# Fewer bursts of zero matmuls, wider routing steps, and two reorderings in an attention-then-experts kernel

## The chip, the cores and the metric

One core of a Trainium2 chip. The metric is device time in microseconds (us). The kernel before took 813.58 us (median of 4 runs, 812.43 to 816.94) beside the changed one. Later runs were on other chips, where the same kernel before took 829.9, 811.6 and 817.0 us; kernels are compared within one chip, or by their ratios to the kernel before on their own chip. Ratios are the mean time of one kernel's fast runs over that of the other's of the same rounds, so not quite the ratio of the medians quoted.

## The reference

```python
# q, k, v: (8 batches, 8 heads, 576 positions, 64)
scores = q @ k.T / 8                 # heads 0-3: last 32 positions; heads 4-7: every 4th of the last 128
attn = softmax(masked scores) @ v    # -> x: (8, 576, 512)
logits = x @ w_gate                  # 8 experts
local  = sigmoid(x @ w_local)
for each batch, for s in order:
    e = argmax(logits[s]) if s == 0 or local[s] < 0.5 else previous e
    out[s] = softmax(logits[s])[e] * (relu(x[s] @ w1[e]) @ w2[e])
```

The choice of an expert is carried from one position to the next, so the routing of a group of two batches is a chain of small steps. The 4608 tokens are then sorted by expert into tiles of 128.

## The kernel before

TensorE's order is set by the program; the other engines' instructions are placed by a scheduler. An outer loop goes over 32 pairs of heads: scores on TensorE (`sc`), a clamp with the mask on VectorE and an exponential on ScalarE (`pr`), value matmuls (`pv`), a scaling on VectorE (`x`), and after every second pair nine transposes (`tp`). A pair's values have 32 positions in common with the block before; VectorE copies them inside the tile once its load has landed (`overlap`). After eight pairs a group is routed: logits, then small steps, each started when a counter of TensorE's work in us (`gap`) has moved on far enough. Forty expert tiles follow.

```python
def overlap(n):
    vt = loaded[n][2]
    nc.vector.tensor_copy(vt[:WIN, :, 1:], vt[QB:, :, :NB - 1])

def idle(times):                 # a burst: products of zeros that nobody reads
    to = bank([P, 4, P], "idle")
    for i in range(times):
        nc.tensor.matmul(to, lhsT=blank, rhs=blank..., start=True, stop=True, ...)

def route(g):
    waiting.extend((us, lambda f=f: f(g)) for us, f in (
        (0.0, logits), (1.5, fresh), (4.0, carry), (1.5, carry_over), (1.0, choose), (2.0, place)))
    # ... table, nine scatters of table entries by GpSimd, then for a table: rows, four tokens() ...

for n in range(NPB + 2):
    if n % 4 == 2 and not begun[0]:   # begun: the experts have
        idle(4)
    if n < NPB:
        scores(n)
        overlap(n)
    gap(1.2); step()                  # step: a part of an expert tile, if one is ready
    if 1 <= n <= NPB:
        values(n - 1) ...
    # ... turn (transposes), load(n + 3), two weight pieces, store ...
```

The logits of a group use three 32-column strips of the array, 384 positions each; the middle strip's positions come from two batches, so its 384 are two runs of 192, and the second of them came in a second round.

Of the kernel before, what the change touches and what calls it, by code (L numbers as in the profile page):

```python
# [22 lines left out]
P = 128  # L23
B, H, S, DH = 8, 8, 576, 64
D = H * DH
E, F = 8, 1024
DK, FK = D // P, F // P
N = B * S
WIN, DIL = 32, 4
# [8 lines left out]
NPB = B * NP  # L38
# [3 lines left out]
CH = 2  # L42
# [3 lines left out]
GB = 2  # L46
NG = B // GB
# [3 lines left out]
NC = 3  # L51
NQ = GS // NC
LW = 32
# [9 lines left out]
NT = CAP + E - 1  # L63
PADS = E * CAP
NOBODY = float(N)

TW = 4

# [121 lines left out]
def whole(ctx, tc, exact, bad, qk, v, wgl, w1, w2, con, msk, qmk, out, cst, wg, ones):  # L190
    nc = tc.nc
# [20 lines left out]
    def bank(shape, name):  # L212
        return banks.tile(shape, F32, name=name, tag="bank")
# [14 lines left out]
    def load(n):  # L228
        kq = ins.tile([P, WIN + 2 * S], F32, name="kq")
        vt = vts[n % len(vts)]  # L230
        nc.sync.dma_start(out=kq, in_=qk[n])
        nc.sync.dma_start(out=vt[WIN:].rearrange("p u i e -> p (u i e)"), in_=v[n])
        loaded[n] = kq[:, :WIN + S], kq[:, WIN + S:], vt
# [5 lines that stand above are left out]
# [5 lines left out]
    def idle(times):  # L244

        if not exact:
            to = bank([P, 4, P], "idle")
            for i in range(times):
                nc.tensor.matmul(to, lhsT=blank, rhs=blank.unsqueeze(1).to_broadcast([P, 4, P]), start=True, stop=True, skip_group_check=True)  # L249
# [18 lines left out]
    nc.vector.memset(fill, 0.0)  # L268
    nc.vector.memset(fill[:, :, 0], NOBODY)
    nc.vector.memset(fill[:, :, 2:], float(ROWS))  # L270
# [64 lines left out]
    def values(n):  # L335

        vt = loaded[n][2]
        if n % 2 == 0:
            xs[n // 2] = xp.tile([P, NB, 2, DH], F32, name="x")
        x = xs[n // 2]  # L340
        for (a, z), pr in zip(UNITS, prob.pop(n)):
            pv = bank([P, z - a, VW], "pv")
            for i in range(a, z):
                for u in range(2):
                    here[:] = [nc.tensor.matmul(pv[u * QB:(u + 1) * QB, i - a],  # L345
                                                lhsT=pr[:, u, (i - a) * QB:(i - a + 1) * QB], rhs=vt[:, u, i],
                                                start=True, stop=True, tile_position=(0, u * QB),
                                                skip_group_check=True)]
            r = rec[:, n, a:z]
            nc.vector.reciprocal(r, pv[:, :, DH])  # L350
            nc.vector.tensor_tensor(x[:, a:z, n % 2], pv[:, :, :DH],  # L351
                                    r.unsqueeze(2).to_broadcast([P, z - a, DH]), op=Alu.mult)
            if not a:
                gap(1.0)
        del loaded[n]
# [17 lines left out]
    def store(m):  # L373

        nc.sync.dma_start(out=xd[m * P * NB:(m + 1) * P * NB].rearrange("(p i) f -> p (i f)", p=P),
                          in_=xs.pop(m).rearrange("p i g d -> p (i g d)"))

    def logits(g):

        st = routes[g]  # L380
        xt = st["xt"]
        lp = bank([P, NQ], "lp")

        pieces = [[(b, c * NQ, max(c * NQ, b * S), min((c + 1) * NQ, (b + 1) * S)) for b in range(GB)
                   if max(c * NQ, b * S) < min((c + 1) * NQ, (b + 1) * S)] for c in range(NC)]
        for r in range(max(map(len, pieces))):
            for kk in range(DK):
                for b, a, s, z in (own[r] for own in pieces if r < len(own)):
                    if kk < CH:
                        rhs = xt[:, 0, s:z, kk]  # L390
                    else:
                        rhs = xt[:, 1, b * S:(b + 1) * S, kk - CH].rearrange("p (c j) -> p j c", c=DIL)
                        rhs = rhs[:, (s - b * S) // DIL:(z - b * S) // DIL]
                    c = a // NQ
                    nc.tensor.matmul(lp[c * LW:(c + 1) * LW, s - a:z - a], lhsT=wg[:, kk], rhs=rhs,
                                     start=(kk == 0), stop=(kk == DK - 1), skip_group_check=True,
                                     tile_position=(0, c * LW))
        st["le"] = le = sm.tile([NC * LW, NQ], F32, name="le")
        nc.scalar.copy(le, lp[:NC * LW])

    def fresh(g):

# [109 lines left out]
    def scatter(g, j):  # L512

        i = nc.gpsimd.indirect_dma_start(  # L514
            out=tab, out_offset=bass.IndirectOffsetOnAxis(ap=routes[g]["places"][:, j:j + 1], axis=0),
            in_=pay[:, g, j], in_offset=None)
        for other in scatters:
            tc.declare_no_dep(i.ins, other.ins, reason="no two tokens have one place")
        for other in table_users + here:
            tc.add_manual_dep(i.ins, other.ins.name, SYNC, reason="comes after")  # L520
        scatters.append(i)
# [67 lines left out]
    def rows(lv):  # L589
        nt = ENDS[lv] - STARTS[lv]  # L590
        ri = tiles["ri", lv]
        tiles["rows", lv] = tr = once.tile([nt, P, TW], F32, name=f"tr{lv}")
        i = nc.gpsimd.indirect_dma_start(
            out=tr.rearrange("t s c -> t (s c)"), out_offset=None, in_=tab.rearrange("(r s) c -> r (s c)", s=P),
            in_offset=bass.IndirectOffsetOnAxis(ap=ri, axis=0))
        for s in scatters:
            tc.add_manual_dep(i.ins, s.ins.name, SYNC, reason="all places")
        table_users.append(i)

    def tokens(lv, c):  # L600

        tr = tiles["rows", lv]
        nt = ENDS[lv] - STARTS[lv]
        what, dtype = (("plain", I32), ("dilated", I32), ("tok", I32), ("gate", F32))[c]
        tp = bank([P, nt], "tt")
        nc.tensor.transpose(tp, tr[:, :, (2, 3, 0, 1)[c]], ident[:nt, :nt])
        tiles[what, lv] = to = once.tile([P, nt], dtype, name=f"{what}{lv}")
        nc.vector.tensor_copy(to, tp)
        if c == 3:
            named[0] = ENDS[lv]  # L610
# [34 lines left out]
    gaps, sent = [0.0], {}  # L645
# [13 lines left out]
            sent[t] = gaps[0]  # L659

    def ready(t):
        return t in sent and gaps[0] - sent[t] > 4.0

    def features(t):
        x = xg.pop(t)
# [46 lines left out]
    waiting, last = [], [0.0]  # L712

    def gap(us):
        gaps[0] += us
        if waiting and gaps[0] - last[0] >= waiting[0][0]:
            last[0] = gaps[0]
            waiting.pop(0)[1]()

    def route(g):  # L720
        waiting.extend((us, lambda f=f: f(g)) for us, f in (
            (0.0, logits), (1.5, fresh), (4.0, carry), (1.5, carry_over), (1.0, choose), (2.0, place)))
        lv = GROUPS.index(g + 1) if g + 1 in GROUPS else None
        if lv is not None:
            waiting.append((1.0, lambda: table(lv)))
        waiting.extend((1.2 if j else 1.5, lambda j=j: scatter(g, j)) for j in range(NJ))
        if lv is not None:
            waiting.append((0.0, lambda: rows(lv)))
            waiting.extend((0.0 if c else 9.0, lambda c=c: tokens(lv, c)) for c in range(4))
            waiting.extend((1.2, lambda t=t, kk=kk: begin(t, kk))  # L730
                           for t in range(STARTS[lv], min(STARTS[lv] + 3, ENDS[lv])) for kk in range(DK))

    def begin(t, kk):
        if t < 3 or t - 3 in turned:
            gather(t, kk)
        else:
            waiting.insert(0, (0.0, lambda: begin(t, kk)))
# [21 lines left out]
    begun = [0]  # L759

    def step():

        t = begun[0] // 3
        if t < LAST and (begun[0] % 3 or ready(t)):
            begun[0] += 1
            next(work_of_experts)
            return True
        return False

    for n in range(NPB + 2):  # L770
        if n % 4 == 2 and not begun[0]:
            idle(4)
        if n < NPB:
            (scores_exact if exact else scores)(n)
            overlap(n)
        gap(1.2)
        step()
        if 1 <= n <= NPB:
            values(n - 1)
            gap(0.8)  # L780
            step()
        if n >= 2 and n % 2 == 1:
            turn((n - 3) // 2)
            if n >= 3 and (n - 3) // 2 % (2 * GB) == 2 * GB - 1:
                route((n - 3) // 2 // (2 * GB))
            gap(0.8)
        if n + ahead < NPB:
            load(n + ahead)
        fetch(2 if not begun[0] else 6)
        if n >= 3 and n % 2 == 1:  # L790
            store((n - 3) // 2)
        step()
# [85 lines left out]
```

## Time and profile before

| what | us |
|---|---|
| span of the profiled run | 808.8 |
| TensorE busy | 767.3 |
| of it zero matmuls | 33.4 |
| attention, routing of groups 0 and 1, first weights | 0 to 182 |
| experts, with what remains of attention | 182 to 797 |

The prediction shows the main lines. Four more, from TensorE's timeline (start, length, instruction, count), are wanted later: the first group's logits, 32 instructions in 4.29 us; the transposes and the burst ahead of pair 14; and the scores right after the last burst, at full speed.

```profile
50.26 4.29 PE L395 MATMUL lp<-xt,wg 128*32 128x384 f32 x32
...
78.51 1.87 PE L368 MATMUL tp<-cst,x 128*128 128x128 f32 x9
80.22 3.60 PE L249 MATMUL idle<-blank 128*128 128x512 f32 x8
...
163.22 1.75 PE L292 MATMUL sc<-kq 64*96 64x64 f32 x36
```

### The profile page before, as it was taken

The numbers are of one execution on the slowest core, as the hardware profiler recorded it, in microseconds if no ns is written. First come the engines' busy times: TensorE is split into PE (matmuls) and PEld (weight loads), VectorE is DVE, ScalarE is ACT, GpSimd is POOL, SyncE is SP. The second block draws the span as 40 slices with busy tenths as digits, with TensorE's granted clock in tenths as the row PEclk, the third lists the DMA queues.
The fourth block names the chain that finished last, engine by engine and source line by source line (L and its number), as shares of the span: only waits on it lengthen the run. The fifth ranks groups of instructions, "written<-read, shape, count | busy, mean of one in ns | idle before, by whom it ended". The sixth has DMA issues, their size and how long they took to land. (4 is left out here: it accounts for less than half of the span.)

```text
span 808.8 us, 15935 instructions
## 1 busy us (share of the span) xinstructions
PE 767.3 (95%) x6060; PEld 566.9 (70%) x6060; DVE 188.1 (23%) x492; ACT 115.3 (14%) x201; POOL 231.3 (29%) x245
## 2 busy tenths in 40 slices
PE   8998899779999997999999999999999999999993
PEld 5767657567777675777677776776867768677681
DVE  5757545451412320110011101110011100111000
ACT  2433322321110110001000000010000100001000
POOL 1001201223363253530333423324233242332200
PEclk9998997899999998999999999999999999999997
DMA  8766846993169197167128311771111841440000
GB/s 317 266 224 199 226 177 172 305 391 121 53 140 364 49 254 215 44 208 271 33 71 305 130 40 30 228 253 37 43 30 44 306 163 43 149 135 28 27 26 19
DMA packets 37032, 124.06 MB, mean 153 GB/s; under 512 B 7955, under 2 KB 8083, under 8 KB 36944
## 3 DMA queue, kind: packets, MB, share of 16 engines
q1 hardware_dynamic: 27152, 101.92, 37.7%
q0 software_dynamic: 9792, 20.99, 9.6%
q8 instruction: 52, 0.85, 0.4%
q14 instruction: 36, 0.29, 0.1%
HBM read 207.90 MB, written 20.88 MB: 283 GB/s over the span
## 5 line engine op out<-in xcount | busy, mean ns | idle before, releaser
L681 PEld LDWEIGHTS hp<-xe,w1s 128*128 128x128 f32 x2560 | 296.0, 194 | 20.6 <-issue 18.5
L681 PE MATMUL hp<-xe,w1s 128*128 128x128 f32 x2560 | 299.5, 277 | 2.3 <-DVE bad L806 1.5
L696 PE MATMUL yp<-w2s,h 128*128 128x512 f32 x640 | 282.1, 593 | 0.0
L696 PEld LDWEIGHTS yp<-w2s,h 128*128 128x128 f32 x640 | 118.2, 190 | 133.0 <-issue 133.0
L652 POOL DMA_INDIRECT xg<-xd,plain x80 | 77.1, 964 | 256.0 <-PE yp L696 240.8
L685 ACT ACTIVATE h<-hp 128x512 f32<-128x512 f32 x80 | 47.8, 597 | 525.2 <-PE hp L681 525.2
L652 POOL DMA_INDIRECT xg<-xd,dilated x80 | 75.5, 943 | 71.1 <-PE yp L696 57.2
L703 DVE TENSOR_SCALAR y<-yp,gate 128x512 f32<-128x512 f32 x40 | 30.0, 750 | 243.2 <-PE yp L696 144.3
L671 DVE COPY xe<-tp 128x512 f32<-128x512 f32 x40 | 27.7, 692 | 237.4 <-PE tp L669 237.4
L514 POOL DMA_INDIRECT tab<-cst,pi x36 | 34.7, 965 | 143.6 <-PE sc L292 80.4
L292 PEld LDWEIGHTS sc<-kq 64*96 64x96 f32 x1152 | 54.7, 169 | 11.9 <-issue 6.1
L704 POOL DMA_INDIRECT out_dram<-y,tok x40 | 40.2, 1004 | 76.8 <-DVE y L703 59.6
L292 PE MATMUL sc<-kq 64*96 64x64 f32 x1152 | 59.8, 256 | 1.0 <-DVE pr L299 1.0
L299 DVE SCALAR_TENSOR_TENSOR pr<-sc,mk 96x640 f32<-96x640 f32 x64 | 47.9, 751 | 53.6 <-PE sc L292 34.6
L302 ACT ACTIVATE pr<-pr 96x640 f32<-96x640 f32 x64 | 43.5, 683 | 117.7 <-DVE pr L299 114.8
L345 PE MATMUL pv<-vt,pr 96*64 96x65 f32 x1152 | 43.7, 232 | 0.0
L345 PEld LDWEIGHTS pv<-vt,pr 96*64 96x64 f32 x1152 | 38.7, 144 | 2.7
L249 PE MATMUL idle<-blank 128*128 128x512 f32 x62 | 33.4, 688 | 2.4 <-DVE blank L242 2.4
L368 PE MATMUL tp<-cst,x 128*128 128x128 f32 x144 | 24.1, 303 | 9.7 <-DVE x L351 9.3
L238 DVE COPY vt<-vt 32x1040 f32<-32x1040 f32 x32 | 22.5, 702 | 24.9 <-DMA vt<-in_v_dram 24.3
L669 PE MATMUL tp<-cst,xg 128*128 128x128 f32 x160 | 25.0, 276 | 3.2 <-DMA xg<-xd,dilated 3.2
L368 PEld LDWEIGHTS tp<-cst,x 128*128 128x128 f32 x144 | 17.1, 153 | 13.8 <-issue 7.5
(109 smaller groups left out, 182.7 us busy)
## 6 DMA issues: line engine op xcount, KB each, us to landing
w1s<-in_w_dram SPq DMA_DIRECT2D x160, 512.0 KB
w2s<-in_w_dram SPq DMA_DIRECT2D x160, 512.0 KB
kq<-in_qk_dram SPq DMA_DIRECT2D x32, 592.0 KB
vt<-in_v_dram SPq DMA_DIRECT2D x32, 292.5 KB
xd<-x SPq DMA_DIRECT2D x16, 576.0 KB
xg<-xd,plain POOLq DMA_INDIRECT x80, 2.9
xg<-xd,dilated POOLq DMA_INDIRECT x80, 3.4
out_dram<-y,tok POOLq DMA_INDIRECT x40, 2.8
```

Source lines behind the costliest of these rows:

```text
L249: nc.tensor.matmul(to, lhsT=blank, rhs=blank.unsqueeze(1).to_broadcast([P, 4, P]), start=True, stop=True, skip_group_check=True)
L292: here[:] = [nc.tensor.matmul(sc[:KW, u, (i - a) * QB:(i - a + 1) * QB], lhsT=kt[h, i * QB:i * QB + KW], rhs=qt[h, i * QB:(i + 1) * QB], s ...
L299: nc.vector.scalar_tensor_tensor(pr[:, :, :w], sc[:KW, :, :w], -CEIL, mk[:, at:at + w].unsqueeze(1).to_broadcast([KW, 2, w]), Alu.max, Alu ...
L302: nc.scalar.activation(pr[:, :, :w], pr[:, :, :w], Act.Exp, scale=SCALE)
L345: here[:] = [nc.tensor.matmul(pv[u * QB:(u + 1) * QB, i - a], lhsT=pr[:, u, (i - a) * QB:(i - a + 1) * QB], rhs=vt[:, u, i], start=True, s ...
L368: nc.tensor.transpose(tp[:, i].rearrange("p u q -> p (u q)"), x[:, c * w + i].rearrange("p g d -> p (g d)"), ident)
L514: i = nc.gpsimd.indirect_dma_start(out=tab, out_offset=bass.IndirectOffsetOnAxis(ap=routes[g]["places"][:, j:j + 1], axis=0), in_=pay[:, g ...
L652: i = nc.gpsimd.indirect_dma_start(out=xg[t][:, kk], out_offset=None, in_=xd if full == ROWS else xd[:full], in_offset=bass.IndirectOffset ...
L681: here[:] = [nc.tensor.matmul(hp[:, m], lhsT=w1s[t % 2][:, half * FK // 2 + m, kk], rhs=x[:, kk], start=(kk == 0), stop=(kk == DK - 1))]
L685: nc.scalar.activation(ht[t][:, half * FK // 2:(half + 1) * FK // 2], hp, Act.Relu)
L696: here[:] = [nc.tensor.matmul(yp, lhsT=h[:, m], rhs=w2s[t % 2][:, m], start=(m == 0), stop=(m == FK - 1))]
L704: nc.gpsimd.indirect_dma_start(out=out, out_offset=bass.IndirectOffsetOnAxis(ap=of_tile("tok", t), axis=0), in_=y, in_offset=None, bounds_ ...
```

## The change

Its intent: drop four of the seven bursts; give the steps of routing, and the row transposes of the last table, more TensorE work between them so that TensorE need not wait; copy the shared values one pair later, when their load has surely landed; and have all logits parts of one weight chunk side by side. It also lets an expert tile begin only when 6.0 us of TensorE's work, in place of 4.0, have passed since its gathers were issued (`ready`).

```diff
+BURSTS = (2, 14, 22)
 # logits: two banks; for each chunk all four parts, in place of two rounds
+        for kk in range(DK):
+            for lp, b, c, s, z in sorted(parts, key=lambda p: p[0] is lps[1]):
 ...
-        nc.scalar.copy(le, lp[:NC * LW])
+        for lp, b, c, s, z in parts:
+            w = slice(c * LW, (c + 1) * LW)
+            nc.scalar.copy(le[w, s - c * NQ:z - c * NQ], lp[w, s - c * NQ:z - c * NQ])
 ...
-        return t in sent and gaps[0] - sent[t] > 4.0
+        return t in sent and gaps[0] - sent[t] > 6.0
 ...
-            (0.0, logits), (1.5, fresh), (4.0, carry), (1.5, carry_over), (1.0, choose), (2.0, place)))
+            (0.0, logits), (2.0, fresh), (4.5, carry), (2.2, carry_over), (1.2, choose), (3.0, place)))
 ...
-            waiting.extend((0.0 if c else 9.0, lambda c=c: tokens(lv, c)) for c in range(4))
+            waiting.extend((0.0 if c else 12.0 if g == NG - 1 else 9.0, lambda c=c: tokens(lv, c)) for c in range(4))
 ...
-        if n % 4 == 2 and not begun[0]:
+        if n in BURSTS:
             idle(4)
+        if 1 <= n <= NPB:
+            overlap(n - 1)
         if n < NPB:
             (scores_exact if exact else scores)(n)
-            overlap(n)
```

## The prediction

> **What bounds the kernel now.** I read the page first, then a table of stretches, then TensorE's own timeline inside the bad stretches, then VectorE's rows beside them. The page says TensorE:

> ```profile
> PE 767.3 (95%) x6060; PEld 566.9 (70%) x6060; DVE 188.1 (23%) x492; ACT 115.3 (14%) x201; POOL 231.3 (29%) x245
> ...
> L249 PE MATMUL idle<-blank 128*128 128x512 f32 x62 | 33.4, 688 | 2.4 <-DVE blank L242 2.4
> ```

> Of the span of 808.8 us, 41.5 are idle on TensorE, and 33.4 of the busy ones are L249, products of zeros that nobody reads: 31 matmuls, each two instructions, as 3 at the start and 7 bursts of 4. The page's average hides where that lies, so next the stretches (columns: us, busy of PE, PEld, DVE, ACT, POOL, granted clock, DMA share, GB/s):

> ```profile
> 2.40:31.40 29.00, 27.94 (x429) 20.70 (x429) 20.05 (x45) 9.58 (x17) 1.39 (x3) 1.00 0.97 341
> 31.40:50.30 18.90, 17.79 (x319) 14.30 (x320) 12.96 (x30) 8.11 (x16) 0.00 (x0) 1.00 0.77 259
> 58.10:83.80 25.70, 23.02 (x329) 18.79 (x328) 16.43 (x59) 8.54 (x15) 2.96 (x3) 0.87 0.61 182
> 110.30:138.00 27.70, 25.01 (x331) 20.10 (x330) 18.26 (x76) 8.40 (x15) 1.92 (x2) 0.82 0.59 166
> 138.00:157.50 19.50, 14.30 (x307) 13.17 (x307) 11.89 (x27) 7.32 (x13) 7.38 (x8) 0.94 0.98 294
> 157.50:182.00 24.50, 20.20 (x280) 14.66 (x279) 11.57 (x28) 6.57 (x12) 6.33 (x7) 0.85 1.02 394
> 182.00:309.00 127.00, 127.00 (x921) 92.86 (x922) 32.89 (x121) 16.77 (x32) 53.30 (x55) 0.99 0.56 170
> 309.00:325.00 16.00, 10.51 (x68) 9.44 (x67) 1.52 (x5) 0.60 (x1) 4.75 (x5) 0.79 0.48 158
> ```

> From 182 us on (the experts) TensorE is full (470.07 of the 472 us from 325 on, by the same view), but for one hole at 309 to 325; the change can win nothing else there. The first 182 us are the attention pairs with the routing of the first two groups: two stretches of routing at a clock of 0.87 and 0.82, and from 138 us DMA at a share of 0.98 to 1.02 while the first weights load. TensorE's timeline shows the pieces (start, length, what, idle before it and its releaser):

> ```profile
> 31.39 3.67 PE L249 MATMUL idle<-blank 128*128 128x512 f32 x8
> 35.00 1.75 PE L292 MATMUL sc<-kq 64*96 64x64 f32 x36
> ...
> 65.69 0.17 PE L450 MATMUL last<-cst,run 9*1 9x9 f32 x1 [1.16 <-DVE rec L350]
> ...
> 71.70 0.41 PE L500 MATMUL kp<-oh,cst 128*128 128x72 f32 x2 [1.29 <-DVE oh L474]
> ...
> 73.28 3.15 PE L292 MATMUL sc<-kq 64*96 64x64 f32 x36
> ...
> 156.88 0.87 PE L368 MATMUL tp<-cst,x 128*128 128x128 f32 x3 [4.89 <-DVE x L351]
> 157.54 5.75 PE L249 MATMUL idle<-blank 128*128 128x512 f32 x8
> ...
> 318.60 0.30 PE L606 MATMUL tt<-cst,tr 32*128 32x32 f32 x1 [5.49 <-DMA tr<-tab,ri]
> ```

> To see: a burst holds TensorE from 31.39 to 35.00. Each routing step has a wait of over 1 us for VectorE, and after it the same 36 score matmuls take 3.15 instead of 1.75: the clock has dropped. At 151.99 to 156.88 TensorE waits for VectorE, which itself waited:

> ```profile
> 154.70 0.69 DVE L238 COPY vt<-vt 32x1040 f32<-32x1040 f32 x1 [4.38 <-DMA vt<-in_v_dram]
> ```

> So VectorE's copy of shared values stood in front of the softmax work, waiting for a load.

> [...]

> **The change part by part.**

> Bursts. They stood ahead of pairs 2, 6, 10, 14, 18, 22, 26; 2, 14 and 22 stay. The one ahead of pair 6 costs 35.00 - 31.39 = 3.61, of 10 58.12 - 54.48 = 3.64, of 18 110.26 - 106.63 = 3.63: 10.9 us. The one ahead of 26 (157.54 to 163.22, 5.68, partly at half clock) is counted with its stage below. Does TensorE use the room? Two pairs cost it 7.6 us without a burst (the scores of pairs 6 and 8 start at 35.00 and 42.63), 0.56 of it a wait. VectorE needs 2 x (0.82 + 0.69 + 0.24 + 0.82 + 0.69) = 6.5. DMA moves 2 x (592 + 292.5) KB in and 576 KB out, 2.4 MB, 7.0 us at 341 GB/s. So TensorE still sets the pace, by little, and the wait has to shrink for that. I give the whole 10.9 and charge new waits below.

> More room between routing steps. The order of TensorE's instructions shows what it makes: the one-column transpose of the carried states moves behind the transposes of x and ten score matmuls (about 2.7 us later), the counting matmuls (kp) by 8 value and 10 score matmuls (about 1.6 us). The waits there are 2 groups x (1.16 + 1.29) = 4.9. The cold work behind them: first group 3.15 - 1.75 in the scores, 2.22 - 1.27 in the value matmuls next to them, about 0.4 in the transposes, 2.8; second group, by the same comparison row by row, 4.4. In all 12.1 us. But the bursts used to give VectorE a rest just before; now it has 4 pairs x 3.26 and some 4.6 of routing operations against TensorE's about 16.6, so it is short by a little, and the bursts kept ahead of 14 and 22 stand just where the clock used to be low. I take 5.5 of 12.1.

> Copy a pair later. In the built order it moves for real only for some pairs (7 to 11, 20, 22, 27). Behind late copies lie waits of 0.79 and 1.81 us and a logits at 5.47 instead of 4.29: 3.8 us; I take 2. The copy for pair 26, whose 4.38 is the worst, keeps its place, so I leave that wait standing.

> Weights stage, pairs 22 to 30. It is limited by DMA: 16 weight pieces of 512 KB, 8 pairs and 4 stores, some 18 MB, 46 to 52 us at 394 to 341 GB/s, after about 134 us. Taking each load's arrival from its place in the queue, scores of pair 30 can start some 42 us after the burst of 22 begins; before, the first expert matmul began 181.85 - 134.2 = 47.6 us after it, with 4.0 us spent waiting for gathered rows (2.37 + 0.79 + 0.83). Without the burst of 26 the experts begin about 46 after it, but with one more pair done (scores 1.67, values 1.2, transposes 1.4): 1.6 + 4.3 = 5.9, and 1.1 of the 1.9 that the first expert matmuls lost to a cold clock (5.67 against 3.8). I take 7.

> Last table's rows (12 in place of 9). The wait of 5.49 us, and then about 1.7 of cold matmuls. In the new order the row transposes come 3.2 us later after the counting than before; the scatters of table entries, which GpSimd issues at 1.27 us each, move with the counting. So some 2.3 of wait remains: 3.2 less, and little of the cold. I take 3.

> Logits side by side. Nothing. The second round of 192 columns already runs beside the first: read instruction by instruction, its first starts at 52.34 while the 384-wide ones of the first round still start until 53.65, and both end within 0.1 us (4.29 us in all). The 384-wide chain sets it: 4 x 0.34 + 4 x 0.67 (strided half) = 4.0. Sorted anew, that chain is the same. ScalarE copies 4 small pieces for one of 0.47: an estimate of 1.3 in all from its 0.47 at 384 columns, hidden by the 1.7 us of scores before the transposes.

> New waits: DMA near 0.95 where it was 0.77 (0.77 x 18.9 / 15.3), VectorE short in routing: -3.

> Sum: 10.9 + 5.5 + 2 + 7 + 3 + 0 - 3 = 25.4. 813.7 - 25.4 = 788.3.

> **The rivals.** First: the bursts were free, since TensorE would have waited for DMA anyway. For it: share 0.97 in the first 31 us, 1.0 from 138. Against: 0.77, 0.61 and 0.59 in between, where three of the four removed ones lie, and at 31.67 the copy found its data there. It would leave some 12 us: 800. Second: the clock. Without zeros, attention's thin matmuls sag to half clock, as they do at 73 and 124 us. Against: from 16.5 to 31.4 and from 35 to 50 no burst stands, and the clock is 1.00. It would cost 3 to 5 us a stretch: 797 or more. Third: everything works, both routings stay warm, the weights stage loses its 4.89 and the row wait goes: 12 more, 776.

> **Range and chances.** The firm part is the 10.9; of the other terms each could be off by 3 to 5 us. 2% is 16.3 us, a time of 797.4, and my centre lies 9 below. Range 778 to 800. Faster 0.76, same 0.22, slower 0.02.

> **What would show it.** L249 with 30 instructions in place of 62. Score matmuls following transposes with no 3.6 us between at pairs 6, 10, 18, 26. Waits at L450's and L500's successors under 0.5 us and their stretch's clock above 0.9 (if not: VectorE is the bound there). The logits still 4.3 us. The wait near the copy of pair 26 still some 4 us. The row transposes waiting 2 to 3 us. First expert matmul at about 160. Experts' last 470 us the same. I am wrong if DMA waits eat the bursts' room, or the clock in 16 to 60 us falls below 0.95.

## The result, and the profile after

786.97 us (median of 4 runs, 782.7 to 787.57), a ratio of 0.9655 with a 95% interval of 0.9611 to 0.9699. The page of the changed kernel: 20 us less of TensorE's busy time, the same share.

```profile
span 785.0 us, 15890 instructions
...
PE 747.0 (95%) x6028; PEld 558.2 (71%) x6028; DVE 187.9 (24%) x492; ACT 118.8 (15%) x213; POOL 231.7 (30%) x245
```

TensorE has 6060 - 6028 = 32 instructions fewer: the 16 matmuls of four bursts. The same table of stretches as before (us, busy of PE, PEld, DVE, ACT, POOL, clock, DMA share, GB/s): the two early routings, the weights stage in three pieces, the last table.

```profile
51.70:73.40 21.70, 20.27 (x330) 15.90 (x328) 17.21 (x61) 9.73 (x19) 2.34 (x2) 1.00 0.69 218
...
97.60:119.30 21.70, 20.30 (x333) 16.13 (x330) 19.13 (x78) 9.67 (x19) 0.96 (x1) 1.00 0.62 202
...
131.00:143.00 12.00, 7.28 (x81) 6.35 (x81) 5.68 (x14) 3.40 (x6) 0.92 (x1) 0.56 1.02 269
143.00:156.60 13.60, 13.60 (x158) 12.61 (x157) 6.17 (x17) 4.04 (x7) 1.01 (x1) 0.51 1.02 413
```

The routing stretches have a clock of 1.00 where it was 0.87 and 0.82. The last row is new and odd: TensorE busy in all of 13.60 us, and the clock at 0.51. TensorE's timeline of the changed kernel, for the places shown of before:

```profile
47.50 4.32 PE L397 MATMUL lp<-xt,wg 128*32 128x384 f32 x32
...
62.66 0.36 PE L464 MATMUL cp<-over,ones 1*128 1x9 f32 x2 [0.56 <-DVE ends L456]
...
65.31 0.41 PE L504 MATMUL kp<-oh,cst 128*128 128x72 f32 x2
...
142.20 0.87 PE L370 MATMUL tp<-cst,x 128*128 128x128 f32 x3 [3.66 <-DVE x L353]
143.00 3.15 PE L294 MATMUL sc<-kq 64*96 64x64 f32 x36
...
154.72 1.95 PE L370 MATMUL tp<-cst,x 128*128 128x128 f32 x9
156.61 1.75 PE L294 MATMUL sc<-kq 64*96 64x64 f32 x36
...
287.52 0.27 PE L610 MATMUL tt<-cst,tr 32*128 32x32 f32 x1 [2.78 <-DMA tr<-tab,ri]
```

The counting matmuls (`kp`) no longer wait, and the carried states cost 0.56 in place of 1.16. The logits are as long as they were. The row transposes (`tt`) wait 2.78 in place of 5.49. And the wait near the copy for pair 26 is still there, with half clock before and behind it (132.4 to 156.3 us, and back without a burst); VectorE's row shows the same cause, a late load:

```profile
140.02 0.69 DVE L240 COPY vt<-vt 32x1040 f32<-32x1040 f32 x1 [5.45 <-DMA vt<-in_v_dram]
```

Where the 23.8 us between the two profiled spans lie (the medians of all runs differ by 26.6), from starts of the same instructions in both traces (a stretch's length before, less its length after):

| stretch | before | after | won |
|---|---|---|---|
| start to scores of pair 2 | 16.49 | 16.75 | -0.3 |
| to the first logits (burst of 6 gone) | 33.77 | 30.75 | 3.0 |
| to scores of pair 10 (burst of 10 gone) | 7.86 | 4.25 | 3.6 |
| to scores of pair 14 (first routing) | 25.63 | 21.64 | 4.0 |
| to the second logits (late copies) | 17.48 | 18.93 | -1.5 |
| to scores of pair 18 (burst of 18 gone) | 9.03 | 5.34 | 3.7 |
| to scores of pair 22 (second routing) | 27.71 | 21.62 | 6.1 |
| to the seventh tile's first layer (weights stage; burst of 26 gone) | 156.96 | 156.00 | 1.0 |
| to the eighth tile's second layer (last table) | 30.8 | 26.6 | 4.2 |
| to the end | 483.1 | 483.1 | 0.0 |

### The profile page after: what moved, and what is told of

It is laid out like the page before. It is cut to its first block, busy times and chain, and to the rows that moved or that the text cites. A ratio compares the mean times of both kernels' runs of the same rounds, so it can differ in the third digit from the quotient of the medians.

```text
span 785.0 us, 15890 instructions
## 1 busy us (share of the span) xinstructions
PE 747.0 (95%) x6028; PEld 558.2 (71%) x6028; DVE 187.9 (24%) x492; ACT 118.8 (15%) x213; POOL 231.7 (30%) x245
## 5 line engine op out<-in xcount | busy, mean ns | idle before, releaser
L685 PEld LDWEIGHTS hp<-xe,w1s 128*128 128x128 f32 x2560 | 292.4, 192 | 20.6 <-issue 17.4
L685 PE MATMUL hp<-xe,w1s 128*128 128x128 f32 x2560 | 295.0, 276 | 2.6 <-DVE bad L811 1.5
L301 DVE SCALAR_TENSOR_TENSOR pr<-sc,mk 96x640 f32<-96x640 f32 x64 | 47.6, 750 | 39.7 <-PE sc L294 27.3
L240 DVE COPY vt<-vt 32x1040 f32<-32x1040 f32 x32 | 22.6, 707 | 21.1 <-DMA vt<-in_v_dram 20.4
L353 DVE TENSOR_TENSOR x<-pv,rec 128x320 f32<-128x320 f32 x64 | 26.7, 450 | 0.1
## 6 DMA issues: line engine op xcount, KB each, us to landing
vt<-in_v_dram SPq DMA_DIRECT2D x32, 292.5 KB
```

Of the source, the lines that this page charges most:

```text
L301: nc.vector.scalar_tensor_tensor(pr[:, :, :w], sc[:KW, :, :w], -CEIL, mk[:, at:at + w].unsqueeze(1).to_broadcast([KW, 2, w]), Alu.max, Alu ...
L685: here[:] = [nc.tensor.matmul(hp[:, m], lhsT=w1s[t % 2][:, half * FK // 2 + m, kk], rhs=x[:, kk], start=(kk == 0), stop=(kk == DK - 1))]
```

## The experiments

My theory after this: three bursts and the room between routing steps made most of the gain; the logits' order and the later copy made none; in the weights stage the dropped burst of pair 26 was worth nothing because a burst was the thing that ended a spell of half clock. The rivals are with each run.

### The bursts (four runs on one chip, where the kernel before took 829.9 us)

```diff
-BURSTS = (2, 14, 22)
+BURSTS = (2, 6, 10, 14, 18, 22, 26)      # a_bursts7
+BURSTS = (2, 14, 22, 26)                 # a_burst26
+BURSTS = (2,)                            # a_burst2
 # b_bursts3, in the kernel before:
-        if n % 4 == 2 and not begun[0]:
+        if n in (2, 14, 22):
```

> The changed kernel with all seven bursts of zeros put back (pairs 2, 6, 10, 14, 18, 22, 26). Theory 1, the bursts ahead of 6, 10 and 18 are dead time: those three cost 3 x 3.6 = 10.9 us, and the fourth, ahead of 26, is neutral because it brings the halved clock back: 787 + 11 = 798. Rival A, the room would be filled by waits for loads: 787 to 791. Rival B, the fourth is dead time too (5.7): 803.

814.0 us, ratio 0.9831 (0.9771 to 0.9891). It differs from the next kernel, on the same chip, by the bursts of 6, 10 and 18 alone: 814.0 - 801.3 = 12.7 us for three bursts that stand for 10.9. They were dead time, and rival A falls. By the starts of the instructions, 9.8 us of it lie where the three bursts stood; other stretches differ in both directions. Rival B put the ratio at 0.987, inside the interval, so this run does not decide on the fourth burst.

> The changed kernel with one burst more, ahead of pair 26. In the changed kernel the granted clock is 0.50 from 132 to 156 us though TensorE is busy from 142 on, and that costs about 5.3 us on the matmuls of pairs 25 to 27; in the kernel before the same burst, at half clock, took 5.7 us and left the clock at 1.00. Theory 1: neutral, within 1.5 us of 787, with the clock at 1.00 from about 148 us on. Rival: thin matmuls recover on their own in time, the burst is dead, 791 to 793.

801.3 us, ratio 0.9662 (0.9607 to 0.9717). The changed kernel did not run on this chip; on two others its ratio was 0.9655 and 0.9717, a spread of 5 us, so the times agree with theory 1 but cannot tell 1.5 us from 5. The nearest comparison on the chip is a_burst2 below, which lacks this burst: from scores of pair 22 to the seventh tile it took 169.1 us, this kernel 168.0. The timeline agrees:

```profile
144.60 0.87 PE L370 MATMUL tp<-cst,x 128*128 128x128 f32 x3 [4.04 <-DVE x L353]
145.27 4.88 PE L251 MATMUL idle<-blank 128*128 128x512 f32 x8
150.09 1.75 PE L294 MATMUL sc<-kq 64*96 64x64 f32 x36
```

After a wait of 4.04 the zeros take 4.88 (3.6 at full clock), and the scores behind them 1.75. In the changed kernel the same scores took 3.15 after the same kind of wait, and row by row the matmuls from 142 to 156 us there are 5.3 us longer than at full clock. What the burst costs, it gives about back. The rival is half right: with thin matmuls alone the clock was back too, at 156.3 us.

> The kernel before with nothing changed but its bursts, at pairs 2, 14 and 22 alone. Theory 1: it gets the three bursts' 10.9 us and loses some to routing waits, which have less time there: 813.6 - 10 = 803 to 805. Rival, the bursts are all of the gain and the other parts are idle: 787 to 790. Rival, without the rest for VectorE that the bursts gave, the close routing steps eat the gain: 809 to 814.

820.6 us, ratio 0.9922 (0.9856 to 0.9987): 6.5 us won of the kernel before by the ratio, 9.3 by the medians. The first rival falls. Theory 1 (0.987 to 0.989) and most of the last rival's range (0.994 to 1.000) both lie inside the interval, so the run does not choose between them. The bursts alone are a quarter to a third of the 28.6 us between the kernel before and a_burst26 on this chip; without the wider steps the routing waits stay (1.2, 1.1 and twice 1.3 us in its list of waits), and its rows wait 11.2 us in two places.

> The changed kernel without the bursts ahead of 14 and 22, so with the one ahead of pair 2 alone. The clock at both places is 1.00 now, before the burst as well. Theory 1, the routing steps no longer let the clock fall, so these two bursts are dead time as well: 787 - 7 = 780, less what loads then make TensorE wait: 780 to 784. Rival, they hold the clock up: it falls to 0.5 after the second or first routing and the time is 787 to 795.

797.2 us, ratio 0.9601 (0.954 to 0.9662), as theory 1 said (0.959 to 0.964), 4.1 us under a_burst26, which has the bursts of 14, 22 and 26 more; the intervals overlap. The clock over both routings, bursts gone, is 1.00 (first two rows; routing lies in 58 to 74 and 105 to 122 us), but between them it is at half (last two rows):

```profile
58.00:74.00 16.00, 14.56 (x272) 12.28 (x268) 13.29 (x45) 6.64 (x12) 2.54 (x3) 1.00 0.83 270
105.00:122.00 17.00, 15.83 (x306) 13.74 (x303) 15.71 (x66) 7.95 (x15) 2.06 (x3) 1.00 0.68 216
...
80.00:85.00 5.00, 4.26 (x39) 3.41 (x37) 1.64 (x5) 1.91 (x4) 1.76 (x2) 0.50 0.81 141
85.00:90.00 5.00, 5.00 (x74) 4.76 (x72) 2.39 (x6) 1.37 (x2) 0.96 (x1) 0.50 1.04 225
```

So the changed kernel's bursts ahead of 14 and 22 guard against a fall that no longer comes in the routing itself. Pairs 10 to 14 and 18 to 22 took 18.2 us each, in a_burst26 21.6: each burst's time came off in full. Part of it was lost behind: the clock was at half from 76.9 to 97.3 us, in a_burst26 from 83.0 to 96.7, and pair 14 to the second logits took 25.6 us in place of 23.2. The rival has that much right.

### The parts one by one (four runs on one chip; before 811.6 us)

> The changed kernel itself, once more, so that the partial ones beside it are compared on one chip; the last four kernels ran on a chip where the kernel before took 829.9 us, not 813.6. Both theories: ratio to the kernel before 0.961 to 0.970, as it was.

788.8 us, ratio 0.9717 (0.9673 to 0.9761), a little outside the range expected of the ratio: how much the kernel before loses differs between chips. It is the yardstick for the next three. Its last table won almost nothing: the row transposes waited 4.5 us in place of 2.78, and the stretch took 29.9 us, not 26.6 (30.8 in the kernel before, on the first chip).

```diff
 # a_room_old
-            (0.0, logits), (2.0, fresh), (4.5, carry), (2.2, carry_over), (1.2, choose), (3.0, place)))
+            (0.0, logits), (1.5, fresh), (4.0, carry), (1.5, carry_over), (1.0, choose), (2.0, place)))
 # a_logits_old: two rounds into one bank, one copy, as before
 # a_copy_old
-        if 1 <= n <= NPB:
-            overlap(n - 1)
         if n < NPB:
             (scores_exact if exact else scores)(n)
+            overlap(n)
```

> The changed kernel with the five routing distances of the kernel before (1.5, 4.0, 1.5, 1.0, 2.0). Comparing the two traces stage by stage, the two early routings gave 4.0 and 5.9 us. Theory 1, the room between steps is what did it (the bursts kept ahead of 14 and 22 do not prevent the fall of the clock, they only end it): 9 to 11 us slower than the changed kernel, ratio to the kernel before about 0.978, with waits of 1.2 and 1.3 us at the transposed last column and the counting matmuls, twice each, and the clock below 0.9 there. Rival, the new order of everything else did it: within 3 us of the changed kernel.

800.3 us, ratio 0.9876 (0.9835 to 0.9918): 11.5 us slower than the yardstick, so theory 1. Pairs 10 to 14 take 27.3 us in place of 21.6, pairs 18 to 22 26.4 in place of 21.6. The old waits are back in its timeline, and the same 36 scores at half clock behind them:

```profile
59.05 0.17 PE L454 MATMUL last<-cst,run 9*1 9x9 f32 x1 [1.12 <-DVE run L448]
...
64.57 0.41 PE L504 MATMUL kp<-oh,cst 128*128 128x72 f32 x2 [1.29 <-DVE oh L478]
...
66.66 3.15 PE L294 MATMUL sc<-kq 64*96 64x64 f32 x36
```

No burst stood ahead of the routing there, as none does in the changed kernel: the room decides, not the rest that a burst gives VectorE.

> The changed kernel with the logits in the order of the kernel before and one copy for the four. Theory 1, the queue already ran the second round beside the first, so the order gives nothing: within 2 us of the changed kernel, logits of 4.3 us in the trace as there. Rival, the second round's 4 x 0.32 us per group stood alone: 5 us slower.

788.3 us, ratio 0.9729 (0.9683 to 0.9775): no difference. Its logits, in the old order:

```profile
45.81 4.32 PE L398 MATMUL lp<-xt,wg 128*32 128x384 f32 x32
```

> The changed kernel with the copy of shared values back at its old place, right after the same pair's scores. In the changed kernel the waits behind late copies did not shrink (TensorE waited 9.2 us for the scaled values, 9.3 before; VectorE 20.4 for the load, 24.3 before). Theory 1: without bursts the old place makes VectorE wait for loads earlier, by some 3 us each time; 2 to 6 us slower than the changed kernel. Rival, the copy is idle too: within 2 us.

789.5 us, ratio 0.9739 (0.9695 to 0.9783): 0.7 us slower by the medians, inside the intervals. My guess of 2 to 6 us is a miss, but the run does not test what its rival says either. In its trace VectorE, ScalarE, GpSimd and SyncE go through the same instructions in the same order as in the yardstick, and TensorE's order shows no difference: the scheduler put the copies where they were, whatever their line in the source. So the edit is idle because it changes nothing that is built, and a copy that really comes a pair later was never run. In this repeat VectorE waited 18.3 us for these loads in all, in the yardstick 20.9.

### Why loads are late, and a better version (four runs on one chip; before 817.0 us)

In both kernels loads slow down for some microseconds in several places: the moved rate falls below 100 GB/s and single packets of 4.7 KB take 1 to 2 us, some longer (up to 4.4), in place of 0.18. In the changed kernel that is so from 74 to 82 us and, on and off, from 123 to 136, when GpSimd's scatters of the first two groups (69.6 to 82.4 and 114.2 to 129.5 us) are under way or just over. Not at every scatter: 128 to 133 us moved 331 GB/s. Nor always at a full DMA share: 74 to 78 us moved 31 GB/s at 0.33.

```diff
 # a_scatter_twice, in scatter(g, j)
+        if g == 0 and not exact:
+            nc.gpsimd.indirect_dma_start(out=tab2, ...same places, same entries...)
 # a_fetch1
-        fetch(2 if not begun[0] else 6)
+        fetch(1 if not begun[0] else 6)
 # a_best1
-BURSTS = (2, 14, 22)
+BURSTS = (2,)
-   ... 12.0 if g == NG - 1 ...
+   ... 15.0 if g == NG - 1 ...
 # a_best3: a_best1 and a_fetch1
```

> The changed kernel with each of the first group's nine scatters of table entries issued a second time, into a table that nobody reads (128 rows of 16 bytes each, 18 KB in all; the result stays right). In both kernels, whenever a group's scatters are in flight, the moved rate falls to 90 to 250 GB/s at a full DMA share and single load packets of 4.7 KB take 1 to 2 us in place of 0.18. Theory 1, the scatters slow the loads: the second set stretches the waits ahead of pairs 16 and 17 (7 us lost there between scores of pair 14 and the second logits, against pairs without scatters) by another 4 to 8 us; 4 to 8 us slower than the changed kernel. Rival, it is plain bandwidth that runs out there: 18 KB more are nothing, within 1.5 us.

799.2 us, ratio 0.9785 (0.9711 to 0.9859). It is probably slower than the changed kernel, whose ratios on other chips were 0.9655 and 0.9717 (the second's interval overlaps), but not where I said. From scores of pair 14 to the second logits it took 15.0 us, where the changed kernel took 18.9 and 20.3 in its two profiles; the slow packets were spread over 77 to 111 us and hurt less there. The loss came later: 26.7 us from scores of pair 18 to those of pair 22, in place of 21.6, with a wait of 1.66 for the carried states and half clock behind it; and 14.0 us from scores of pair 26 to those of 27, in place of 5.9, of which 8.1 is a wait for the first table's rows. Most slow packets go with scatters in time, but the size of the waits did not follow their number. What slows the packets stays open.

> The changed kernel with one weight piece fetched per step of the attention loop in place of two, while the experts have not begun. Theory 1, the weights stage is limited by DMA and what falls behind are the pairs' own loads, which stand behind weights in one queue: the waits of 1.5 and 3.7 us near pairs 25 and 26 shrink, the clock stays up, and 4 to 8 us are gained, if the second tile's weights still come in time. Rival, the scatters alone jam these loads: the waits stay, within 2 us. A second rival: the missing weights are waited for at the experts' start, 3 to 10 us slower.

795.0 us, ratio 0.9711 (0.9646 to 0.9775): no gain that shows, and theory 1 misses. Scores of pair 25 to 26 still take 12.3 us (10.9 in the changed kernel), with half the weights in the queue. So the weights' bytes alone did not hold these loads back.

> The changed kernel without the bursts ahead of 14 and 22, and with 15 in place of 12 ahead of the last table's row transposes. Theory 1: the first gave 0.5% on another chip (0.9601 against 0.9655 to 0.9662), the second removes the wait of 2.8 to 4.5 us at those transposes: 6 to 8 us faster than the changed kernel. Rival: the wait only moves to the gathers behind it, and the clock falls in a routing step without its burst: within 2 us.

781.6 us, ratio 0.9573 (0.9499 to 0.9647). The first half of the rival falls: the row transposes do not wait at all, nor do the matmuls behind them.

```profile
285.66 0.27 PE L610 MATMUL tt<-cst,tr 32*128 32x32 f32 x1
```

Pairs 10 to 14 and 18 to 22 took 18.2 us each here too. But pair 25, which the kernel now reaches sooner, waits for its load, and the half clock is there as before:

```profile
130.82 3.14 PE L294 MATMUL sc<-kq 64*96 64x64 f32 x36 [5.83 <-DMA kq<-in_qk_dram]
```

> Both of these, the last two kernels' edits together. Theory 1: their gains add, 10 to 15 us faster than the changed kernel, near 774. Rival: the weights' loads come too late and it is slower than the one without it.

782.8 us, ratio 0.9597 (0.9539 to 0.9655): the same as a_best1, so the two gains do not add and theory 1 misses. Beside a_fetch1, on one chip, it has a_best1's two edits more and is 795.0 - 782.8 = 12.2 us faster. By the starts of its instructions, 4.2 us of it are won by the scores of pair 14, 7.7 by those of pair 22, and another 5.0 between the seventh and the eighth tile. So a_best1 is the fastest by its median: surely faster than the kernel before, and by that pair of runs probably faster than the changed kernel, though it did not run beside the changed kernel itself and their ratios' intervals overlap.

Loading four pairs ahead in place of three, against late loads, was not run.

## Why the prediction was right or wrong, point by point

It said 788.3 us; 786.97 was measured, and 788.8 on another chip. That the total came so near was luck: the room was put 4.6 us too low, the weights stage 6.0 and the copy 3.5 too high, and the errors cancelled.

- **Bursts, 10.9 us.** Right: 3.0 + 3.6 + 3.7 = 10.3 in the trace, 12.7 in the pair of runs. The rival that they were free is refuted.
- **Room between routing steps, 5.5 of 12.1 us.** The mechanism was right, the size was not: 4.0 + 6.1 = 10.1 in the trace, 11.5 in the run that undid it. I halved it for VectorE being short of time and for the bursts kept. VectorE was busy 17.21 of 21.70 and 19.13 of 21.70 us, so nearly the bound in the second, but no longer ahead of a waiting TensorE; and the kept bursts were dead time there (18.2 us without them, 21.6 with them).
- **Copy a pair later, 2 us.** Wrong: the stretch behind lost 1.5 us. I took the copies that stand elsewhere in the built order for the work of this edit; with the edit undone they stand in the same places, so they moved with the other edits. The waits were those of late loads.
- **Weights stage, 7 us.** Wrong: 1.0, and this is the step that failed most. I expected the first expert matmul 46 us after the burst of 22; it came 168.13 - 115.75 = 52.4 after it. Two things in that step failed. I took the queue's rate as 341 to 394 GB/s, but during the scatters and just behind them it was lower (247 in 119.3 to 131.0 us, 269 in 131 to 143). And I left out the clock: behind a wait of 1.47 us for a late load it was at half from 132.4 us, and with no burst ahead of 26 that lasted to 156.3; the part behind 143 cost about 5.3 us, near what the burst would have. My second rival had it as a danger for the stretches of 16 to 60 us, where the clock stayed at 1.00; the place was wrong.
- **Last table, 3 us.** 4.2 in the first trace, with 2.78 of wait in place of the 2.3 that should remain; on the other chip the wait was 4.5 and the gain 0.9 against the first chip's kernel before, so the size is not settled.
- **Logits, nothing.** Right, 788.3 beside 788.8 us, and 4.32 us long in both orders. In the trace of the kernel before, the second round's first 192-column matmul of the middle strip started at 52.34 us, ahead of first-round matmuls of other strips, which started until 53.67: taking the source's order as the program's, different column strips went out of order there, so the new order had nothing to win.
- **New waits, 3 us.** No such term was measured by itself. What fell short elsewhere, 0.6 of the bursts and 1.5 in the late-copy stretch, is of that order.

Of the signs named ahead, all held but one (the first expert matmul at about 160 us): the routing clock above 0.9, the logits at 4.3, the wait near pair 26's copy at 3.66, the row transposes waiting 2 to 3, and the end unchanged.

## What to carry to other kernels

A short wait in a stretch of thin matmuls can cost more than itself, because half clock can come behind it and last for many us with TensorE fully busy (0.51 over 13.60 us in the changed kernel): 2.4 us of waits per routing step chain cost 4 to 6 us here, so spacing dependent small steps was worth more than the sum of their waits. Filler matmuls were dead time here where the clock was up (3.4 us or more each), and about even where it was down (from scores of pair 22 to the seventh tile 168.0 us in a_burst26, 169.1 in a_burst2); once the waits ahead of them are gone, take them out again and look at the granted clock behind them too. Before believing that an edit of the source was tested, compare the order of instructions in the two traces. And before reordering matmuls to run side by side, read in the trace whether they already do.
